# Attention and two feed-forward layers on one core: w_out2 rounded in layer 1, other tile addresses, the tail loaded sooner

## The chip, the core and the metric

The kernel runs on one NeuronCore of a Trainium2 chip, as one program. The time is the device time of one execution in microseconds; three executions of the kernel before took 1527.24, 1527.33 and 1527.49 us (median 1527.33). Beside them stands one profiled execution, from which all rows below come.

## The reference

The reference is a bidirectional softmax attention between tokens and a small state, and behind it two feed-forward layers. All is float32; the weights reach the kernel as 64-bit numbers, seen as pairs of 32-bit words.

```python
B, H, S, Ns, D = 8, 8, 512, 32, 64
xread = softmax(scale * x @ state.T) @ state        # for each of the 8 blocks and 8 heads
sread = softmax(scale * state @ x.T) @ x
x = concatenate([xread, sread], tokens)             # 8 * (512 + 32) = 4352 tokens of 512
h = x @ w_in;  x = maximum(0.01 * h, h) @ w_out     # layer 1, 2048 wide
g = x @ w_gate; x = (silu(g) * (x @ w_val)) @ w_out2   # layer 2, 1536 wide
```

## The kernel before

Every matmul of float32 numbers is made of three products of rounded parts: a number v is split into a high part h (ScalarE's `split_h`, line 161, a cast to fp32r) and a low part l = v - h (VectorE's `split_l`, line 164); `passes` (line 426) adds wl·vh, wh·vl and wh·vh in PSUM. The stationary operand of a matmul is a 128 x 128 tile, the moving one 128 x 512.

**Weights to float32.** `stage` (line 189) loads a tile `ws` of raw 64-bit weights, 512 KB. `to_f32` (line 204) gives six steps: scale and low on ScalarE, sign, limit, join and add on VectorE. `convert` (line 230) runs them over a list of keys, interleaved: for key n it issues scale(n), limit(n-1); low(n), sign(n); join(n-1); add(n-1) and the next load, in four steps, of which each `pump(1)` issues one. `finish2` (line 1080) takes each ready pair of keys of layer 2, makes the sums and splits that layer 2's products need (tiles `hl`, three buffers) and stores them to DRAM; each `pump_finish(1)` issues one of its steps.

**Layer 1** (from line 1296) works on 8 blocks j of 512 tokens and 16 column groups f, one iteration for each (j, f): `h_mm` (line 487), `h_act` (line 505: copy, leaky ReLU `hs`, split into `gh`, `gl`) and `y_mm` (line 524, with the products of two iterations before). Block 0 also converts layer 1's own weights. In blocks 1 to 6 each iteration pumps one step of `convert` and one of `finish2` over 24 keys of w_gate and w_val. The last block also carries the tail, the 256 state tokens, numbered block B: its weights come as `tail_in` and are split into `ch` and `cl` two iterations ahead (lines 1268 and 1272). There each iteration of TensorE is h_mm(B, f+1), h_mm(7, f+2), y_mm(7, f), y_mm(B, f), and six `convert` and five `finish2` steps are pumped. At f = 6 (`Y_SUMS`, line 1399) a loop drains what is left of both, the pool `prep` is closed, and layer 2's tiles are opened in its place: `load_w` fills 16 places `wq`, and `y_sums` (line 588) begins.

**Layer 2** (`layer2`, line 691) works on the 8 blocks in four pairs p. For the hidden values of a pair, seven products in Strassen's manner stand for eight (`quads`, line 752; `product`, line 696: six matmuls on one `wq` place). ScalarE copies the sums `C` out of PSUM and VectorE adds to them. `read_out` (line 866) multiplies the hidden values, split into `zh` and `zl` as stationary tiles, by the moving `wo` tiles of w_out2: 24 steps of 12 matmuls. Between the pairs p = 2 and p = 3 the `tail` (line 896) does the same for the 256 state tokens, with plain products: `hidden` and a read-out per f. w_out2 is converted within pair 0: `convert_o` (line 809) issues one of its four steps per key beside each product, loads the raw rows with two ahead, splits them, and stores the split parts (`wo_dram`) and the whole ones (`w2_dram["o", ...]`), which the tail loads and splits again.

**Order and addresses.** The kernel schedules by hand: each engine runs its instructions in the order in which the code issues them, and an instruction that waits holds all behind it on its engine. All loads and most stores go through SyncE's queue. Tiles of layer 2 come from `Places` (line 573), lists of named places; `take` asks for tiles aligned to 128 bytes.

In the built program of before, the sixteen `wq` places lie at byte 195072 and on, 2048 or 2176 apart; divided by 256, eight of their addresses leave 128 and eight leave 0. `zh` and `zl` leave 160. Layer 1's stationary tiles leave 128.

Of the kernel before, what the change touches and what calls it, by code (L numbers as in the profile page):

```python
# [9 lines left out]
F32 = mybir.dt.float32  # L10
# [15 lines left out]
def kernel(  # L26
# [123 lines left out]

    HF = NF2 // 2
    w2_dram = {
        (k, f): dram.tile([P, 2, 512], F32, name=f"w2_{k}{f}") for k in ("gate", "val", "o") for f in range(HF)
# [50 lines left out]
    def to_f32(key):  # L204
        t = staged.pop(key)
# [9 lines left out]
            "limit": lambda: nc.vector.tensor_scalar(  # L215
# [5 lines left out]
            "add": lambda: nc.vector.tensor_tensor(out=v, in0=v, in1=low3, op=ALU.add),  # L221
# [351 lines left out]
    class Places:  # L573
# [117 lines left out]
    def layer2(p2, ps2):  # L691
# [117 lines left out]
        def convert_o():  # L809

            places = {}

            def load(f):
                if f < NF2:
                    t, places[f] = wo_places.take("ws", [P, 512, 2], I32)
                    stage(("o", f), rows(w_out2, f), None, t)

            load(0)
            load(1)
            yield  # L820
            for f in range(NF2):
                v, tag = temps.take("raw")
                raw["o", f] = v
                ops = to_f32(("o", f))
                ops["scale"]()
                ops["low"]()
                ops["sign"]()
                yield
                ops["limit"]()
                ops["join"]()  # L830
                yield
                ops["add"]()
                wo_places.give(places.pop(f))
                hl, hl_tag = wo_places.take("hl")
                split_h(hl[:, 0].bitcast(F32R), v)
                load(f + 2)
                yield
                nc.sync.dma_start(out=w2_dram["o", f // 2][:, f % 2], in_=v)
                split_l(hl[:, 1].bitcast(F32R), v, hl[:, 0])
                yield  # L840
                nc.sync.dma_start(out=wo_dram[f // 2][:, f % 2], in_=hl)
                wo_places.give(hl_tag)
                temps.give(tag)

# [51 lines left out]
        def tail():  # L896
            n = widths[B]
            y = []
            for k in range(2):
                t, tag = temps.take("yr")  # L900
                nc.sync.dma_start(
                    out=t.rearrange("p (k c) -> p k c", k=2), in_=y_dram[B][:, 2 * k:2 * k + 2, :]
                )
# [6 lines left out]
            order = [(key, f) for f in range(NF2) for key in ("gate", "val", "o")]  # L910
            loads = iter(order)
            raw2 = {}

            def load2():
                key = next(loads, None)
                if key:
                    kind, f = key
                    a, b = (f // 2, f % 2) if kind == "o" else (f % HF, f // HF)
                    raw2[key] = wtiles[0].take("wraw")
                    nc.sync.dma_start(out=raw2[key][0], in_=w2_dram[kind, a][:, b])  # L920

            parts2 = {}
# [31 lines left out]

            for _ in range(4):
                load2()
            yield
            for kind in ("gate", "val"):
                split2(kind, 0)
                yield  # L960
# [507 lines left out]
```

## Time and profile before

| | |
|---|---|
| median of three runs | 1527.33 us |
| the profiled execution, its own time | 1526.71 us |
| its span, first to last instruction | 1524.9 us |
| TensorE busy | 1481.4 us (97%), 7114 matmuls |
| VectorE busy | 954.8 us (63%) |
| ScalarE busy | 688.7 us (45%) |
| GpSimd busy | 3.0 us, 8 instructions |
| granted TensorE clock, mean | 0.993 |
| stages | layer 1 to 702.7 us; pair 0 to 910, pair 1 to 1094, pair 2 to 1280, tail to 1337, pair 3 to the end |

In the profile's rows PE is TensorE, ACT ScalarE, DVE VectorE, POOL GpSimd and SP SyncE; "SPq" is its DMA queue. L432 is a line of the kernel; `out<-in` are the tiles that an instruction writes and reads. Times are from the span's start. A matmul's own time overlaps that of the next, so the pace is read from runs of many. In a row of waits, what ended the wait stands behind the arrow.

### The profile page before, as it was taken

What the parts mean: (1) busy time and instruction counts of PE and PEld (TensorE: products, weight loads), DVE (VectorE), ACT (ScalarE), POOL (GpSimd) and SP (SyncE); (2) the same over time, 40 slices, a digit from 0 to 9 for tenths busy, and PEclk for the clock granted to TensorE, in tenths of its full rate; (3) what the DMA queues carried; (4) which work ended last, traced back from release to release, by engine and by line L of the source; (5) the groups of instructions that cost most, each with busy time, mean ns of one, the idle gap of its engine ahead of it and who ended that gap; (6) DMA issues with size and microseconds to landing.
All of it is one profiled execution on the core that took longest, in us unless ns stands there. A gap on an engine that the chain in (4) does not pass through costs nothing.

```text
span 1524.9 us, 20092 instructions
## 1 busy us (share of the span) xinstructions
PE 1481.4 (97%) x7114; PEld 1158.6 (76%) x7114; DVE 954.8 (63%) x1728; ACT 688.7 (45%) x1246; POOL 3.0 (0%) x8
## 2 busy tenths in 40 slices
PE   6999999999999999999879999999999998999999
PEld 2446777777778778887658888888888887988887
DVE  6888688787877777865864534455344554744442
ACT  6777555555554545545433332333223333533322
POOL 0000000000000000000000000000000000000000
PEclk9999999999999999999999999999999999999999
DMA  8885444445453545664898666667666377576345
GB/s 296 291 302 173 139 153 158 145 173 178 135 176 116 190 138 183 249 218 167 297 309 301 224 235 202 190 214 238 224 190 189 101 242 251 180 257 191 118 146 186
DMA packets 146164, 307.53 MB, mean 202 GB/s; under 512 B 14608, under 2 KB 35088, under 8 KB 145040
## 3 DMA queue, kind: packets, MB, share of 16 engines
q1 hardware_dynamic: 144912, 297.85, 59.2%
q10 hardware_dynamic: 1152, 8.39, 1.3%
q8 instruction: 57, 0.93, 0.3%
q14 instruction: 43, 0.35, 0.1%
HBM read 228.59 MB, written 77.59 MB: 201 GB/s over the span
## 4 chain that ended last, share of the span: by engine, by line
PE 50%; DMA 4%; DVE 3%; ACT 1%; issue 1%; SPq 0%; ACTq 0%; DVEq 0%
PE ps_o L432 18%; PE ps_x L708 16%; PE ps_s L708 8%; PE ps_a L708 4%; PE ps_t L432 2%; PE ps_y L432 1%; DMA wo<-hl 1%; DMA ws<-in_dram 1%; PE ps_h L432 1%; DMA yr<-y_dram 1%; PE ps_yt L432 1%; DVE C L724 0%; DMA wraw<-w_gate 0%; ACT sg L728 0%; DVE hl L164 0%
## 5 line engine op out<-in xcount | busy, mean ns | idle before, releaser
L432 PE MATMUL ps_y<-gh,w_parts 128*128 128x512 f32 x1024 | 338.9, 391 | 0.0
L708 PE MATMUL ps_x<-yc,wq 128*128 128x512 f32 x1152 | 286.5, 396 | 14.9 <-DVE C L724 8.4
L708 PEld LDWEIGHTS ps_x<-yc,wq 128*128 128x128 f32 x1152 | 217.0, 189 | 67.9 <-DVE C L724 11.0
L432 PE MATMUL ps_o<-wo,zh 128*128 128x512 f32 x768 | 241.8, 396 | 0.0
L432 PEld LDWEIGHTS ps_y<-gh,w_parts 128*128 128x128 f32 x1024 | 192.2, 188 | 51.7 <-issue 8.1
L432 PE MATMUL ps_y<-gl,w_parts 128*128 128x512 f32 x512 | 199.5, 390 | 0.2 <-DVE gl L164 0.2
L432 PEld LDWEIGHTS ps_o<-wo,zh 128*128 128x128 f32 x768 | 144.3, 188 | 35.1
L432 PE MATMUL ps_o<-wo,zl 128*128 128x512 f32 x384 | 151.6, 395 | 2.4 <-DVE zl L164 2.4
L708 PE MATMUL ps_s<-yc,wq 128*128 128x512 f32 x576 | 149.6, 395 | 2.5 <-ACT C L720 2.5
L164 DVE TENSOR_TENSOR zl<-z,zh 128x512 fp32r<-128x512 f32 x96 | 66.3, 691 | 117.9 <-ACT zh L161 117.9
L161 ACT CAST gh<-hs 128x512 fp32r<-128x512 f32 (+1 forms) x144 | 85.9, 597 | 114.7 <-DVE hs L515 114.6
L164 DVE TENSOR_TENSOR gl<-hs,gh 128x512 fp32r<-128x512 f32 (+1 forms) x144 | 95.3, 662 | 57.4 <-ACT gh L161 54.6
L708 PEld LDWEIGHTS ps_s<-yc,wq 128*128 128x128 f32 x576 | 108.5, 189 | 27.9 <-ACT C L720 3.3
L161 ACT CAST zh<-z 128x512 fp32r<-128x512 f32 x96 | 59.1, 620 | 143.9 <-PE ps_o L432 143.8
L515 DVE SCALAR_TENSOR_TENSOR hs<-hs 128x512 f32<-128x512 f32 (+1 forms) x144 | 94.4, 656 | 31.3 <-ACT hs L514 30.2
L728 ACT ACTIVATE sg<-C 128x512 f32<-128x512 f32 x72 | 45.5, 632 | 148.1 <-DVE C L724 144.2
L514 ACT COPY hs<-ps_h 128x512 f32<-128x512 f32 (+1 forms) x144 | 80.5, 559 | 70.4 <-PE ps_h L432 69.2
L432 PEld LDWEIGHTS ps_y<-gl,w_parts 128*128 128x128 f32 x512 | 96.2, 188 | 20.1 <-DVE gl L164 0.5
L432 PE MATMUL ps_h<-ah,swl 128*128 128x512 f32 x256 | 106.5, 416 | 1.7 <-ACT hs L514 1.2
L432 PE MATMUL ps_h<-al,swh 128*128 128x512 f32 x256 | 100.4, 392 | 0.0
L432 PE MATMUL ps_h<-ah,swh 128*128 128x512 f32 x256 | 100.2, 391 | 0.0
L724 DVE TENSOR_TENSOR C<-ps_s,C 128x512 f32<-128x512 f32 x48 | 33.1, 690 | 106.0 <-PE ps_s L708 105.4
(128 smaller groups left out, 2023.8 us busy)
## 6 DMA issues: line engine op xcount, KB each, us to landing
wo<-wo SPq DMA_DIRECT2D x96, 512.0 KB, 4.5
wq<-quad_gate SPq DMA_DIRECT2D x168, 256.0 KB, 3.1
wq<-quad_val SPq DMA_DIRECT2D x168, 256.0 KB, 3.2
ws<-in_dram SPq DMA_DIRECT2D x68, 512.0 KB, 4.5
sw_dram<-sw SPq DMA_DIRECT2D x56, 256.0 KB, 3.0
sw<-sw_dram SPq DMA_DIRECT2D x56, 256.0 KB, 3.7
quad_gate<-hl SPq DMA_DIRECT2D x24, 512.0 KB, 4.5
quad_val<-hl SPq DMA_DIRECT2D x24, 512.0 KB, 4.1
```

The source lines that it names most:

```text
L161: nc.scalar.copy(dst, src)
L164: nc.vector.tensor_tensor(out=dst, in0=src, in1=hi.bitcast(F32), op=ALU.subtract)
L432: nc.tensor.matmul(ps, lhsT=w, rhs=v, start=first and n == 0, stop=last and n == len(todo) - 1)
L514: nc.scalar.copy(hs, ps[:, :n])
L515: nc.vector.scalar_tensor_tensor(out=hs, in0=hs, scalar=0.01, in1=hs, op0=ALU.mult, op1=ALU.max)
L708: nc.tensor.matmul(bank, lhsT=a, rhs=v, start=first and n == 0, stop=last and n == len(todo) - 1, skip_group_check=True,)
L724: nc.vector.tensor_tensor(out=kept[0], in0=bank, in1=kept[0], op=ALU.add)
L728: nc.scalar.activation(t[0], c, AF.Sigmoid)
```

## The change

w_out2's twelve row blocks become keys `("o", f)` at the end of layer 2's list in layer 1, so that `convert` and `finish2` handle 36 keys; the six row pairs get a branch of their own in `finish2`, which only splits and stores. `convert_o` and the whole parts in DRAM go. For layer 2's keys the steps limit and add run on GpSimd. Two pumps come twice as often. `Places` no longer aligns; a pad of 96 bytes ahead of `wpool`'s places, and the free choice in `p2`, give other addresses: in the built program all `wq` places, and `zh` and `zl`, now leave 128 over 256. The tail loads its input `yr` and its first weights at the start of pair 2's read-out, keeps three keys loaded ahead instead of four, and loads w_out2's two parts split.

```diff
@@ to_f32
+        engine = nc.vector if key[0] in ("in", "out") else nc.gpsimd
...
-            "limit": lambda: nc.vector.tensor_scalar(
+            "limit": lambda: engine.tensor_scalar(
...
-            "add": lambda: nc.vector.tensor_tensor(out=v, in0=v, in1=low3, op=ALU.add),
+            "add": lambda: engine.tensor_tensor(out=v, in0=v, in1=low3, op=ALU.add),
@@ Places.take
-            align = None if self.pool.space == bass.MemoryType.PSUM else 128
-            t = self.pool.tile(shape or self.shape, dtype, tag=tag, name=name, bufs=1, align_bytes=align)
+            t = self.pool.tile(shape or self.shape, dtype, tag=tag, name=name, bufs=1)
@@ quads
-        def quads(f, early, beside):
+        def quads(f, early):
             for n, step in enumerate(ORDER2):
-                next(beside, None)
@@
-        def convert_o():
...
@@ tail
+            order = [(key, f) for f in range(NF2) for key in ("gate", "val", "o")]
...
+                if kind == "o":
+                    h, ht = wtiles[0].take("wh", dtype=F32R)
+                    l, lt = wtiles[0].take("wl", dtype=F32R)
+                    for m, t in enumerate((h, l)):
+                        nc.sync.dma_start(out=t.bitcast(F32), in_=wo_dram[f // 2][:, f % 2, m])
+                    parts2[key] = (h, l), (ht, lt)
...
+            yr = []
+            for k in range(2):
+                yr.append(temps.take("yr"))
...
+            for _ in range(3):
+                load2()
+            yield
...
-            for _ in range(4):
-                load2()
-            yield
@@ layer2, the loop over pairs
-                if f == HF - 1 and not p:
-                    assert next(beside, 0) == 0
+                if f == HF - 2 and not p:
                     load_wo(4)
...
-                others.append(count(tail_steps, 6))
+                others = [count(tail_steps, 1), *others, count(tail_steps, 5)]
@@ the keys of layer 2, and finish2
+        keys2 += [("o", f) for f in range(NF2)]
...
+                if kind == "o":
+                    for n in range(2):
+                        hl = halves().rearrange("p a b c -> p a (b c)")
+                        split_h(hl[:, 0].bitcast(F32R), t[:, n])
+                        yield 1
+                        split_l(hl[:, 1].bitcast(F32R), t[:, n], hl[:, 0])
+                        yield 1
+                        nc.sync.dma_start(out=wo_dram[f // 2][:, n], in_=hl)
+                    finished[0] += 1
+                    continue
@@ layer 1, blocks 1 to 6
-                pump(f % 8 == 4)
-                pump_finish(f % 8 == 0)
+                pump(f % 4 == 2)
+                pump_finish(f % 4 == 0)
@@ the last block, f == Y_SUMS, behind load_w(WQ)
+                    wpool.tile([P, 24], F32, tag="pad", name="pad")
```

The order of instructions shows what this moves. First VectorE at the end of the drain of the last block, from the `cl` of f = 8 on. Before, the drain's rows between the second `gl` and the next `cl` are a few splits:

```order
L164 TENSOR_TENSOR cl<-tail_in,ch 128x512
L515 SCALAR_TENSOR_TENSOR hs<-hs 128x256
L164 TENSOR_TENSOR gl<-hs,gh 128x256
L515 SCALAR_TENSOR_TENSOR hs<-hs 128x512
L164 TENSOR_TENSOR gl<-hs,gh 128x512
L164 TENSOR_TENSOR hl<-hl 128x2x256 x2
L164 TENSOR_TENSOR hl<-two,hl 128x2x256 x2
L164 TENSOR_TENSOR swl<-sw,swh 128x512
L164 TENSOR_TENSOR cl<-tail_in,ch 128x512
```

Now (L215 is the sign, L221 the join, L165 `split_l`), the same `gl` and the eleven rows behind it are these:

```order
L165 TENSOR_TENSOR gl<-hs,gh 128x512
L215 TENSOR_SCALAR two<-ws 128x512
L221 SCALAR_TENSOR_TENSOR two<-ws,two 128x512
L165 TENSOR_TENSOR hl<-two,hl 128x512 x2
L215 TENSOR_SCALAR two<-ws 128x512
L221 SCALAR_TENSOR_TENSOR two<-ws,two 128x512
L215 TENSOR_SCALAR two<-ws 128x512
L165 TENSOR_TENSOR hl<-two,hl 128x512
L221 SCALAR_TENSOR_TENSOR two<-ws,two 128x512
L165 TENSOR_TENSOR hl<-two,hl 128x512
L215 TENSOR_SCALAR two<-ws 128x512
L221 SCALAR_TENSOR_TENSOR two<-ws,two 128x512
```

It goes on in this manner up to the next `cl`: 9 rows of L215, 10 of L221, 12 splits and a `swl` stand between that `gl` and that `cl`.

Second, SyncE in the same place, up to the first load of `yr` for layer 2. Before, it stores the last sums:

```order
L1119 DMA quad_gate_131<-hl 128x1024 x2
L1091 DMA w_val_119<-two 128x1024
L1263 DMA tail_in<-win_dram_106 128x4x128
L1109 DMA quad_val_137<-hl 128x1024
L1112 DMA quad_val_137<-hl 128x1024
L1119 DMA quad_val_137<-hl 128x1024 x2
L594 DMA yr<-y_dram_95 128x512
```

Now the loads of raw w_out2 (L194) and the stores of its parts (L1073) stand there in turns:

```order
L1104 DMA quad_val_131<-hl 128x1024 x2
L1248 DMA tail_in<-win_dram_106 128x4x128
L194 DMA ws<-in_dram 128x1024 x2
L1073 DMA wo_132<-hl 128x1024 x2
L194 DMA ws<-in_dram 128x1024 x2
L1073 DMA wo_133<-hl 128x1024 x2
L194 DMA ws<-in_dram 128x1024 x2
L1073 DMA wo_134<-hl 128x1024 x2
L194 DMA ws<-in_dram 128x1024 x2
L1073 DMA wo_135<-hl 128x1024 x2
L1073 DMA wo_136<-hl 128x1024 x2
L1073 DMA wo_137<-hl 128x1024 x2
```

All stores of w_out2's parts, and eight of its twelve loads, have moved behind layer 1's last stores of sums.

Third, ScalarE at the start of layer 2, from its first copy C. Before, the steps of w_out2 stand between the copies:

```order
L720 COPY C<-ps_x 128x512
L210 ACTIVATE ws<-ws 128x512
L211 ACTIVATE ws<-ws 128x512
L720 COPY C<-ps_s 128x512
L161 CAST hl<-raw 128x512
L720 COPY C<-ps_x 128x512
```

Now the copies follow each other:

```order
L722 COPY C<-ps_x 128x512
L722 COPY C<-ps_s 128x512
L722 COPY C<-ps_x 128x512
L722 COPY C<-ps_s 128x512
L722 COPY C<-ps_x 128x512
```

The 36 instructions of ScalarE for w_out2 have left pair 0.

## Rows read from the trace of the kernel before

**Rows 1.** The page's first part: busy time, share and instructions of each engine.
```profile
PE 1481.4 (97%) x7114; PEld 1158.6 (76%) x7114; DVE 954.8 (63%) x1728; ACT 688.7 (45%) x1246; POOL 3.0 (0%) x8
```

**Rows 2.** Waits of TensorE: who waited for whom, us in total, times, longest.
```profile
PE ps_x L708 <- DVE C L724: 8.4, 6, 3.2
...
PE ps_x L708 <- ACT C L720: 6.5, 2, 4.8
PE ps_t L432 <- DVE wl L164: 3.4, 1, 3.4
PE ps_h L432 <- DVE cl L164: 3.0, 3, 1.9
PE ps_s L708 <- ACT C L720: 2.5, 1, 2.5
...
PE ps_o L432 <- DVE zl L164: 2.4, 1, 2.4
```

**Rows 3.** The chain that ended last, in order of time: start, us, what.
```profile
657.58 3.06 PE ps_h L432 x18
...
674.82 2.72 PE ps_y L432 x12
...
681.80 2.72 PE ps_y L432 x12
...
702.73 1.40 PE ps_x L708 x6
...
845.57 64.44 PE ps_o L432 x276
...
1029.19 64.45 PE ps_o L432 x276
```

**Rows 4.** Groups of ScalarE from 704 to 800 us: busy, mean ns, idle before.
```profile
L210 ACT ACTIVATE ws<-ws 128x512 f32<-128x512 f32 x12 | 8.0, 669 | 13.3 <-DMA ws<-in_dram 13.3
...
L161 ACT CAST hl<-raw 128x512 fp32r<-128x512 f32 x12 | 7.4, 620 | 28.9 <-DVE raw L221 28.9
```

**Rows 5.** The chain from 1115 to 1142 us, in pair 2.
```profile
1121.38 1.38 PE ps_a L708 x6
1122.77 1.40 PE ps_x L708 x6
1124.17 1.37 PE ps_s L708 x6
```

**Rows 6.** SyncE's timeline from 1255 us; then a stretch's busy times, clock, DMA.
```profile
1282.26 0.73 SPq L920 DMA_DIRECT2D wraw<-w_o  x1
...
1283.00:1297.00 14.00, 10.63 (x58) 9.84 (x58) 7.89 (x16) 5.34 (x12) 0.00 (x0) 0.76 0.66 227
```

**Rows 7.** Timeline of VectorE from 622 us: start, us, what.
```profile
622.53 0.42 DVE L515 SCALAR_TENSOR_TENSOR hs<-hs 128x256 f32<-128x256 f32 x1
622.87 0.68 DVE L218 SCALAR_TENSOR_TENSOR two<-ws,two 128x512 int32<-128x512 int32 x1
623.47 0.42 DVE L164 TENSOR_TENSOR gl<-hs,gh 128x256 fp32r<-128x256 f32 x1
```

**Rows 8.** Groups of GpSimd over the span.
```profile
L1320 POOL MEMSET zero<- 128x512 f32 x1 | 0.5, 526 | 550.1 <-PE ps_r L399 550.1
masks.py:199 POOL TENSOR_SCALAR_AFFINE_SELECT ident<-ident 128x128 f32<-128x128 f32 x1 | 0.3, 292 | 0.1
masks.py:197 POOL MEMSET ident<- 128x128 f32 x1 | 0.2, 204 | 0.0
```

**Rows 9.** The page's DMA issues: KB each, median us to landing.
```profile
ws<-in_dram SPq DMA_DIRECT2D x68, 512.0 KB, 4.5
...
wo<-hl SPq DMA_DIRECT2D x12, 512.0 KB, 6.1
```

**Rows 10.** Timelines of VectorE and of TensorE behind the drain of before.
```profile
639.76 0.68 DVE L164 TENSOR_TENSOR cl<-tail_in,ch 128x512 fp32r<-128x512 f32 x1
...
643.12 0.69 DVE L164 TENSOR_TENSOR gl<-hs,gh 128x512 fp32r<-128x512 f32 x1 [0.68 <-ACT gh L161]
...
640.59 0.35 PE L432 MATMUL ps_h<-tailh,cl 128*128 128x256 f32 x1 [1.94 <-DVE cl L164]
```

More of the change, by code (lines that the diff above doesn't have):

```diff
@@ L152 @@
     w2_dram = {
-        (k, f): dram.tile([P, 2, 512], F32, name=f"w2_{k}{f}") for k in ("gate", "val", "o") for f in range(HF)
+        (k, f): dram.tile([P, 2, 512], F32, name=f"w2_{k}{f}") for k in ("gate", "val") for f in range(HF)
     }
@@ L807, in load_wo @@
                     nc.sync.dma_start(out=t.bitcast(F32), in_=wo_dram[f // 2][:, f % 2])
-        def convert_o():
[L811 to L819, printed above, removed]
-            yield
[L821 to L843, printed above, removed]
         zs = {}
@@ L897, in tail, with load2 @@
             n = widths[B]
+            order = [(key, f) for f in range(NF2) for key in ("gate", "val", "o")]
+            loads = iter(order)
+            raw2, parts2 = {}, {}
+            def load2():
+                key = next(loads, None)
+                if not key:
+                    return
+                kind, f = key
+                if kind == "o":
[4 more added lines that the diff above has]
+                    parts2[key] = (h, l), (ht, lt)
+                else:
+                    raw2[key] = wtiles[0].take("wraw")
+                    nc.sync.dma_start(out=raw2[key][0], in_=w2_dram[kind, f % HF][:, f // HF])
+            yr = []
+            for k in range(2):
+                yr.append(temps.take("yr"))
+                nc.sync.dma_start(
+                    out=yr[k][0].rearrange("p (k c) -> p k c", k=2), in_=y_dram[B][:, 2 * k:2 * k + 2, :]
+                )
+            for _ in range(3):
+                load2()
+            yield
             y = []
             for k in range(2):
[L900 to L903, printed above, removed]
+                t, tag = yr[k]
                 parts = wres.tile([P, 2, 2 * n], F32R, tag=f"wr{14 + k}", name="yt", bufs=1)
@@ L909, in tail @@
                 yield
[L910 to L922, printed above, removed]
             def split2(kind, f):
                 if f < NF2:
-                    t, tag = raw2.pop((kind, f))
-                    h, ht = wtiles[0].take("wh", dtype=F32R)
-                    l, lt = wtiles[0].take("wl", dtype=F32R)
-                    split_h(h, t)
-                    split_l(l, t, h)
-                    wtiles[0].give(tag)
+                    if kind != "o":
+                        t, tag = raw2.pop((kind, f))
+                        h, ht = wtiles[0].take("wh", dtype=F32R)
+                        l, lt = wtiles[0].take("wl", dtype=F32R)
+                        split_h(h, t)
+                        split_l(l, t, h)
+                        wtiles[0].give(tag)
+                        parts2[kind, f] = (h, l), (ht, lt)
                     load2()
-                    parts2[kind, f] = (h, l), (ht, lt)
             def hidden(f):
@@ L996, in first_z @@
                 split_z(f, h)
-        beside = convert_o()
         for p in range(len(pairs)):
@@ L1064, in next_load2 @@
                 k, f = key = loads2.pop(0)
-                stage(key, columns(w_gate if k == "gate" else w_val, f), prep)
+                stage(key, rows(w_out2, f) if k == "o" else columns(w_gate if k == "gate" else w_val, f), prep)
         twos, finished = [], [0]
```

3 lines of the change are left out of this document (1 added, 2 removed).

## The prediction

> **What bounds the kernel now.** The page's first part comes first: TensorE is busy for 1481.4 of 1524.9 us [rows 1], so a change can take away only what TensorE waits, or what each of its matmuls is too slow, and it can add waits. The waits of TensorE [rows 2] lie in three places. The first quarter of layer 2 waits for C, the copies and sums of ScalarE and VectorE: 8.4 + 6.5 + 2.5 = 17.4 us. The last block of layer 1 waits 3.0 us for cl, the low part of a tail weight, a VectorE result. The tail's start waits 3.4 us for wl and 2.4 us for zl. The chain in order of time [rows 3] then dates the stages: block pair 0 of layer 2 runs from 702.73 to 845.57 + 64.44 = 910.01, block pair 1, which has the same matmuls, from there to 1029.19 + 64.45 = 1093.64. All numbers are of this one execution of 1526.7 us; the median of the runs is 0.6 us above it. A measurement of this kernel can tell about 0.2%, 3 us, from no change.
>
> **Part 1: w_out2 leaves layer 2.** Pair 0 takes 207.3 us, pair 1 183.6 us. In pair 0 ScalarE's scale step waited 13.3 us for the loads of raw w_out2 and its casts 28.9 us for VectorE [rows 4], each time with copies of PSUM queued behind it. The order of ScalarE at the start of layer 2 shows that after the change only those copies are left. Bounds: the 17.4 us of named waits, and the whole difference of 23.7. I take -23, since pair 1 runs without one wait under the same load that pair 0 will then have.
>
> **Part 2: addresses.** Three products of six matmuls follow each other at 1121 to 1126 us, on the places at bytes 220800, 222976 and 225152 of the kernel before. Divided by 256 these leave 128, 0 and 128, and the products take 1.38, 1.40 and 1.37 us [rows 5]; eight of the sixteen places are of each kind. In layer 1 the stationary weights all leave 128, and twelve matmuls take 2.72 us, 0.227 each [rows 3]. In the read-out zh and zl leave 160, and 276 take 64.45 us, 0.2335 each. After the change all of them leave 128. Pair 1 without its 288 read-out matmuls is 183.6 - 67.2 = 116.4 us for 504, 0.231 each. With 0.228, as the 1.37 us say, 2016 matmuls gain 5.8 us; with 0.227, 1152 of the read-out gain 7.8. Bounds: nothing, if the address is not the cause, and 2016 x 0.004 + 7.8 = 16 us if all reach layer 1's pace. I take -13.5.
>
> **Part 3: the tail sooner.** The load of yr, and zl behind it, no longer ends late: 2.4 us. The other wait, 3.4 us, had a load that SyncE issued at 1282.26 or later, behind the stores of the read-out [rows 6]. The order of SyncE after the change has the load of val 1 behind these stores, and hidden(1) needs it soon, so this wait stays with another tile. The stretch from 1283 to 1297 has a granted clock of 0.76 [rows 6], 14 x 0.24 = 3.4 us lost at the lower level, 1.2 GHz; whether that goes with the smaller gap is open. Bounds: 0 and 2.4 + 3.4 + 3.4 = 9 us. I take -3. The o parts come split, 512 KB instead of 256 KB a step, under a steady 4.25 us of TensorE; I cost that at nothing, covered by the 3 steps of loading ahead.
>
> **Part 4: w_out2 and GpSimd in layer 1.** There are now 36 keys where there were 24. Through blocks 1 to 6 they are spread out, a step or two in each iteration. The place that matters is the last block at f = 6, where what is left is drained in one go. In the order of VectorE before, five instructions stood between a gl and the next cl; now 32: 9 signs, 10 joins, 12 splits (every one of w_out2) and a swl. TensorE needs that cl. Its queue holds behind it everything else of layer 1, and one step of 681.80 - 674.82 = 7.0 us in front of it [rows 3].
>
> How long is the drain? VectorE alone: short instructions follow each other at 0.34 us and long ones at 0.60 [rows 7], so with that cl 9 x 0.34 + 24 x 0.60 = 17.5 us. But a key's chain is longer. GpSimd's limit and add have no row. Its affine select, which reads and writes 128 elements, takes 0.29 us, a memset of 128 0.20 and one of 512 0.53 [rows 8]. The memsets give 0.10 us fixed, so an operation with one input at 512 is (0.29 - 0.10) x 4 + 0.10 = 0.88 us, and a second input adds 4 x 0.09, so 1.23 us. Bounds: 0.53 for either, and four times 0.29 for the limit, twice that for the add.
>
> In the drain key n + 1's sign stands ahead of key n's join, and key n + 1 is loaded into the buffer that the add of key n - 2 gives free. So from an add to the second one after it: load 4.5 us to landing [rows 9], scale 0.67 [rows 4], sign 0.42, join 0.68, add 1.23, and 0.2 for handing over: 7.7 us for two keys. The first two adds need no new load and end at 2.3 and 5.0 us; the ninth then ends at 2.3 + 4 x 7.7 = 33, the tenth 2.8 later (limit, join, add), then a cast 0.62 [rows 4], a split, swl and cl: 38.5 us. The stores of hl (three buffers, 6.1 us to landing [rows 9]) give 3 keys in some 10.7 us, about the same pace.
>
> The drain starts after the gl that ended 3.4 us behind the cl before [rows 10]; TensorE has 7.0 us to do. Wait: 3.4 + 38.5 - 7.0 = 34.9 us. What the same stretch loses now goes away: from 640.59 - 1.94 = 638.65, where TensorE could have begun [rows 10], to 657.58 [rows 3], two steps of 7.0 took 18.9 us, so 5. A wait of this length will leave TensorE at 1.2 GHz for a while, as the stretch after 1283 does [rows 6]: 2 us. Net +32. Bounds: with 17.5 us +11; with 50 us, rival 2, some +44. The limit and add of the other keys I cost at +1.5, from 0, if what VectorE no longer does covers them, to 8.
>
> Sum: -23 - 13.5 - 3 + 32 + 1.5 = -6. 1526.7 - 6 + 0.6 = **1521 us**.
>
> **Rivals.** *1, the drain is short.* If loads and stores keep ahead, the drain is VectorE's 17.5 us, part 4 becomes +11 + 1.5, and the time 1500. For it: most of the first keys' data is there when it starts. Against it: in the order of SyncE six of the twelve loads stand behind its stores.
>
> *2, slower: GpSimd and VectorE take turns.* No row of before shows the two at work together, since GpSimd has 8 instructions. If each of its operations kept VectorE out, a drained key would cost 1.9 us of VectorE (sign, join, split), 2.1 of GpSimd and some 1 us of loads not covered: 5 us, the drain 50 us and part 4 +44; the 26 keys before the drain would hold VectorE for another 55 us, of which I let 5 reach TensorE. The time is then 1526.7 - 39.5 + 49 + 0.6 = 1537. It decides from about 4.5 us per key on, where the sum is zero. The Trainium skill states such a rule in "SBUF — State Buffer", section "SBUF: two separate sides": VectorE instructions with two SBUF inputs and GpSimd share a port pair, held for a whole instruction, and the other engine blocks. By that rule, the sum would be the 1537 us just given; no run here shows it yet. The skill's "GPSIMD Engine Reference", section "Performance versus the Vector engine", gives 4497 ns for an add of 2048 elements, a quarter of which, as an estimate, is 1.1 us; with it the sum would be 1 us lower.
>
> *3, the address is not the cause.* Then part 2 is nothing: 1534.5 us. Against it: the pace alternates with the place, product by product, and layer 1 has the faster one throughout.
>
> *4, the change does not do what it says.* If pair 0 stays slow for another reason (the copies themselves), -23 shrinks to -17: 1527.
>
> **How the numbers follow.** Forecast 0.52, with an own range of 1509 to 1531 (8 us on the drain, 3 on the rest); rival 1 0.18; rival 2 0.20; rival 3 0.06; rival 4 0.04. The range takes in rivals 1 and 2 nearly whole: 1502 to 1537. Faster by over 3 us: rival 1 and some three quarters of the forecast, 0.57. Within 3 us: 0.18, from the forecast's upper part and rival 4. Slower: 0.25, rivals 2 and 3.
>
> **What would show it.** Pair 0 within 2 us of pair 1; no wait for C. Read-out runs of 276 at 62.7 us instead of 64.4. In the waits of TensorE one long wait of ps_h for cl near 650 us, some 35 us: under 20 makes part 4 wrong, and rival 1 right. In it, ScalarE waiting for ws and hl (loads, stores) speaks for my chain; VectorE and GpSimd each idle while the other runs, with long rows of GpSimd, for rival 2. One wait of about 3 us at the tail's start. If GpSimd's add takes over 2 us, the step that is wrong is its price.

## The result and the profile after

The kernel after took 1534.8 us (four executions, 1534.35 to 1535.46), the kernel before beside it 1527.41 us: 1.0053 of the time before, 95% interval 1.004 to 1.0067. That is slower by half a per cent, where the prediction had 1521 us and faster. The profiled execution has a span of 1532.6 us, 7.7 us more than before, at a granted clock of 0.981 instead of 0.993.

First the page's part 1 of the kernel after, then its waits of TensorE (us in total, times, longest); they answer to [rows 1, 2]:

```profile
PE 1462.9 (95%) x7114; PEld 1156.8 (75%) x7114; DVE 938.6 (61%) x1644; ACT 681.6 (44%) x1234; POOL 90.1 (6%) x80
```

```profile
PE ps_h L435 <- DVE cl L165: 39.3, 2, 38.9
...
PE ps_t L435 <- DVE wl L165: 6.3, 4, 2.7
PE ps_r L402 <- ACT et L394: 2.7, 2, 2.4
...
PE ps_h L435 <- ACT hs L517: 2.4, 2, 1.8
...
PE ps_y L435 <- ACT yst L558: 1.5, 2, 1.2
PE ps_y L435 <- DVE gl L165: 1.0, 2, 0.8
```

TensorE is busy 18.5 us less: its matmuls are quicker. The waits for C of pair 0 are gone, one long wait for cl has come, the tail waits four times instead of once, and ps_r, ps_h and ps_y wait in blocks 1 to 6, where [rows 2] have almost nothing. The chain in order of time dates the stages, as [rows 3] do for before:

```profile
694.38 5.46 PE ps_h L435 x18
...
749.03 1.39 PE ps_x L710 x6
...
757.22 1.36 PE ps_a L710 x6
...
866.02 62.56 PE ps_o L435 x276
...
1045.54 62.63 PE ps_o L435 x276
```

Layer 2 begins at 749.03 instead of 702.73 us: layer 1 is 46.3 us longer. Pair 0 then takes 866.02 + 62.56 - 749.03 = 179.6 us, pair 1 up to 1045.54 + 62.63 also 179.6; before they took 207.3 and 183.6. Taking each stage from its first matmul to the next one's, layer 1 has +46.3, pair 0 -27.7, pair 1 -4.0, pair 2 -6.3, the tail +3.4 and pair 3 -4.0: together +7.7 us, the difference of the spans.

The n-th matmul is the same in both programs, so the two traces can be laid side by side. At the end of block 6 (matmul 2840 of 7114) TensorE is 7.9 us behind the kernel before; in the last block this grows to 9.8, falls to 6.1 where short waits of the kernel before have no counterpart, is 44.5 right behind the drain's wait, and 46.3 at the start of layer 2. So layer 1's loss has two parts: 9.8 us ahead of the drain, nearly all of it in blocks 1 to 6, and 46.3 - 9.8 = 36.5 at the drain (its wait and the low clock behind it, less the short waits of before).

**The drain.** ScalarE's scale steps in it:

```profile
658.85 0.67 ACT L213 ACTIVATE ws<-ws 128x512 f32<-128x512 f32 x1 [3.45 <-DMA ws<-in_dram]
...
667.46 0.65 ACT L213 ACTIVATE ws<-ws 128x512 f32<-128x512 f32 x1 [2.55 <-DMA ws<-in_dram]
...
676.00 0.65 ACT L213 ACTIVATE ws<-ws 128x512 f32<-128x512 f32 x1 [2.87 <-DMA ws<-in_dram]
...
684.53 0.65 ACT L213 ACTIVATE ws<-ws 128x512 f32<-128x512 f32 x1 [2.97 <-DMA ws<-in_dram]
```

These are every second key, and each waits for its load (between them stands one more such wait): (684.53 - 658.85) / 3 = 8.6 us for two keys. Behind such a load the same turn goes on like this on VectorE (sign, a split, join):

```profile
676.68 0.43 DVE L215 TENSOR_SCALAR two<-ws 128x512 int32<-128x512 int32 x1 [3.55 <-ACT ws L213]
677.02 0.69 DVE L165 TENSOR_TENSOR hl<-two,hl 128x512 fp32r<-128x512 f32 x1
677.62 0.69 DVE L221 SCALAR_TENSOR_TENSOR two<-ws,two 128x512 int32<-128x512 int32 x1
```

From 655 to 694 us no engine is busy for half of the time, VectorE for 16.6, ScalarE for 15.4 and GpSimd for 18.9 of 39 us (the stretch: busy time of PE, PEld, DVE, ACT, POOL, then granted clock, DMA share, GB/s).

```profile
655.00:694.00 39.00, 0.46 (x4) 0.25 (x3) 16.62 (x30) 15.44 (x27) 18.85 (x18) 0.56 0.70 244
```

**Blocks 1 to 6.** GpSimd's groups over the span, then the timelines of GpSimd and of VectorE at one of its adds:

```profile
L224 POOL TENSOR_TENSOR two<-two,ws 128x512 int32<-128x512 int32 x36 | 55.5, 1542 | 438.7 <-ACT gh L162 196.2 <-DVE two L221 170.2 <-ACT hs L517 30.3
L218 POOL TENSOR_SCALAR ws<-ws 128x512 f32<-128x512 f32 x36 | 32.7, 909 | 162.3 <-DVE two L215 162.3
```

```profile
471.08 1.80 POOL L224 TENSOR_TENSOR two<-two,ws 128x512 int32<-128x512 int32 x1 [13.91 <-ACT gh L162]
472.85 1.08 POOL L218 TENSOR_SCALAR ws<-ws 128x512 f32<-128x512 f32 x1
```

```profile
471.03 0.69 DVE L165 TENSOR_TENSOR gl<-hs,gh 128x512 fp32r<-128x512 f32 x1
471.64 1.79 DVE L165 TENSOR_TENSOR hl<-hl 128x512 fp32r<-128x512 f32 x1
473.36 0.67 DVE L338 TENSOR_REDUCE r<-st 128x16 f32<-128x512 f32 x1
```

VectorE's split, 0.69 us in the row above it, takes 1.79 us while GpSimd adds, and GpSimd's add takes 1.80 where the shortest took 1.27. As I read it, each one's time holds the time for which the other held it up. The means fit; VectorE's groups from 160 to 630 us in the kernel after:

```profile
L165 DVE TENSOR_TENSOR gl<-hs,gh 128x512 fp32r<-128x512 f32 x100 | 76.2, 762 | 56.3 <-ACT gh L162 55.5
...
L165 DVE TENSOR_TENSOR al<-a,ah 128x512 fp32r<-128x512 f32 x12 | 10.4, 870 | 0.0
...
L322 DVE TENSOR_REDUCE m<-st 128x16 f32<-128x512 f32 x12 | 8.2, 686 | 0.4
```

and in the first experiment below, which has no GpSimd steps:

```profile
L165 DVE TENSOR_TENSOR gl<-hs,gh 128x512 fp32r<-128x512 f32 x101 | 69.9, 692 | 39.7 <-ACT gh L162 37.4
...
L322 DVE TENSOR_REDUCE m<-st 128x16 f32<-128x512 f32 x12 | 8.2, 686 | 0.4
...
L165 DVE TENSOR_TENSOR al<-a,ah 128x512 fp32r<-128x512 f32 x12 | 8.2, 684 | 0.0
```

These splits, with two inputs in SBUF, got longer, a reduction with one input did not. (Not every two-input group did: the join has 686 and 684 ns.)

**The tail.** SyncE in the kernel after:

```profile
1256.67 29.09 SPq L808 DMA_DIRECT2D wo<-wo  x12
1285.82 0.42 SPq L881 DMA_DIRECT2D wraw<-w_gate  x1
...
1290.06 0.59 SPq L881 DMA_DIRECT2D wraw<-w_val  x1
```

The first three weights are loaded early, but the fourth, gate 1, is issued only at 1285.82 us, behind twelve loads of `wo` that wait for their places, and val 1 behind the read-out's last stores.

### The profile page after: what moved, and what is told of

It is laid out like the page before. It is cut to its first block, busy times and chain, and to the rows that moved or that the text cites. A ratio compares the mean times of both kernels' runs of the same rounds, so it can differ in the third digit from the quotient of the medians.

```text
span 1532.6 us, 20186 instructions
## 1 busy us (share of the span) xinstructions
PE 1462.9 (95%) x7114; PEld 1156.8 (75%) x7114; DVE 938.6 (61%) x1644; ACT 681.6 (44%) x1234; POOL 90.1 (6%) x80
## 4 chain that ended last, share of the span: by engine, by line
PE 50%; DMA 4%; DVE 2%; ACT 1%; issue 1%; POOL 0%; SPq 0%; POOLq 0%; ACTq 0%; DVEq 0%
PE ps_x L710 17%; PE ps_o L435 16%; PE ps_s L710 9%; PE ps_a L710 4%; DMA wraw<-w_gate 2%; PE ps_y L435 1%; PE ps_h L435 1%; DMA ws<-in_dram 1%; PE ps_yt L435 1%; DVE wl L165 1%; DMA wo<-wo 0%; ACT wh L162 0%; POOL two L224 0%; DVE hs L518 0%; DMA wraw<-w_val 0%
## 5 line engine op out<-in xcount | busy, mean ns | idle before, releaser
L710 PE MATMUL ps_x<-yc,wq 128*128 128x512 f32 x1152 | 278.0, 389 | 0.0
L435 PE MATMUL ps_o<-wo,zh 128*128 128x512 f32 x768 | 236.6, 389 | 0.0
L165 DVE TENSOR_TENSOR gl<-hs,gh 128x512 fp32r<-128x512 f32 (+1 forms) x144 | 102.3, 710 | 75.4 <-ACT gh L162 74.0
L710 PE MATMUL ps_s<-yc,wq 128*128 128x512 f32 x576 | 146.1, 389 | 0.0
L165 DVE TENSOR_TENSOR zl<-z,zh 128x512 fp32r<-128x512 f32 x96 | 66.3, 691 | 115.7 <-ACT zh L162 115.7
L518 DVE SCALAR_TENSOR_TENSOR hs<-hs 128x512 f32<-128x512 f32 (+1 forms) x144 | 102.5, 712 | 21.3 <-ACT hs L517 20.1
```

The lines of the kernel that those rows point to most:

```text
L165: nc.vector.tensor_tensor(out=dst, in0=src, in1=hi.bitcast(F32), op=ALU.subtract)
L435: nc.tensor.matmul(ps, lhsT=w, rhs=v, start=first and n == 0, stop=last and n == len(todo) - 1)
L518: nc.vector.scalar_tensor_tensor(out=hs, in0=hs, scalar=0.01, in1=hs, op0=ALU.mult, op1=ALU.max)
L710: nc.tensor.matmul(bank, lhsT=a, rhs=v, start=first and n == 0, stop=last and n == len(todo) - 1, skip_group_check=True,)
```

## The experiments

The medians of the kernel before beside these runs lie between 1524.6 and 1525.5 us; each ratio is to those of its own group of runs.

### Limit and add back on VectorE

```diff
-        engine = nc.vector if key[0] in ("in", "out") else nc.gpsimd
+        engine = nc.vector
```

> The kernel after, with limit and add of layer 2's keys back on VectorE. Layer 1 of the kernel after falls 9.8 us behind the kernel before up to the last block's drain. Theory A, GpSimd's steps hold VectorE up: most of the 9.8 us goes (0 to 3 stay), and the wait of 38.9 us in the last block loses about 1 us in each of its 4 to 5 two-key cycles (an add of 0.7 instead of 1.5 us, a limit of 0.4 instead of 0.6): 1534.8 - 8 - 5 = 1522 us, 1519 to 1526. Rival B, the delay in blocks 1 to 6 comes from the additional conversion steps, whoever runs them: the 9.8 us stay or grow, since VectorE gets 72 more instructions; only the drain gets shorter: 1530 to 1537 us.

Measured: 1516.43 us, ratio 0.9937 (0.9923 to 0.9951). The first row of its waits of TensorE, and two scale steps of ScalarE in its drain, two keys apart:

```profile
PE ps_h L435 <- DVE cl L165: 33.5, 2, 32.7
```

```profile
643.07 0.69 ACT L213 ACTIVATE ws<-ws 128x512 f32<-128x512 f32 x1 [1.58 <-DMA ws<-in_dram]
...
650.65 0.67 ACT L213 ACTIVATE ws<-ws 128x512 f32<-128x512 f32 x1 [2.35 <-DMA ws<-in_dram]
```

Theory A, and by more than it said: at the end of block 6 TensorE is 0.7 us ahead of the kernel before, so the whole lag was GpSimd's doing, although VectorE has 72 instructions more. The denser steps alone, then, cost nothing up to there. The turn of two keys falls from 8.6 to 7.6 us. With the change's GpSimd steps alone undone, it would have been faster than before.

### The drain spread over blocks 1 to 6

```diff
-                pump(f % 4 == 2)
-                pump_finish(f % 4 == 0)
+                pump(f % 2 == 0)
+                pump_finish(1)
```

> The kernel after, with more frequent steps in blocks 1 to 6: the second convert step in every other iteration instead of every fourth, two finishing steps in every iteration; by a count of the steps nothing is left for the drain at f = 6. Theory A, the drain is a chain of loads and stores that TensorE waits for once and that hides when it is spread: the wait of 38.9 us and 3 us of low clock behind it go, and the 10 keys that move forward cost what the other 26 do (9.8 / 26 = 0.4 us each): 1534.8 - 42 + 4 = 1497 us, 1494 to 1506. Rival B, VectorE (busy 64 of 80 us in these blocks) has no room: each key moved costs TensorE its 3 us of VectorE and 2 us of GpSimd, 10 x 5 = 50 us, and the time stays near 1535 to 1543 us.

Measured: 1520.38 us, ratio 0.9968 (0.9955 to 0.998). Neither theory holds alone: the wait for the drain is gone (ps_h for cl is not among the longer waits), but TensorE is 34.1 us behind at the end of block 6. Whose fault that is, VectorE's load or GpSimd, the next three kernels tell.

### The same, with VectorE's steps, and with one of the two on GpSimd

```diff
-        engine = nc.vector if key[0] in ("in", "out") else nc.gpsimd
+        engine = nc.vector
...
+                pump(f % 2 == 0)
+                pump_finish(1)
```

> Both edits together: limit and add on VectorE, and the more frequent steps in blocks 1 to 6. Theory A (the 35 us that layer 1 lost in the kernel with spread steps are GpSimd's doing, and the drain is a chain that hides once spread): nothing of the 35 us in blocks 1 to 6, no drain: from 1516.4 us of the kernel with VectorE's steps its wait of 33.0 us and 2 to 3 us of low clock go, the ten keys moved forward cost 0 to 4: 1480 to 1485 us. Rival B (VectorE has no room for ten more keys in blocks 1 to 6, whoever runs limit and add): 10 keys x 4 us of VectorE cost TensorE up to 40 us there, 1500 to 1520 us.

Measured: 1490.11 us, ratio 0.9771 (0.9756 to 0.9786). Nearest to theory A (1480 to 1485), with more left in blocks 1 to 6 than it said: 6.9 us behind at the end of block 6, and no drain.

With limit alone on GpSimd, in the kernel with spread steps:

```diff
-            "add": lambda: engine.tensor_tensor(out=v, in0=v, in1=low3, op=ALU.add),
+            "add": lambda: nc.vector.tensor_tensor(out=v, in0=v, in1=low3, op=ALU.add),
```

> The kernel with spread steps (1520.4 us), with add on VectorE and only limit on GpSimd. Beside it one with only add on GpSimd. With neither some 1482 us, so there are 38 us to share. Theory A, VectorE is kept out for the whole of any GpSimd instruction: the price goes with GpSimd's busy time (limit 36 x 0.91 = 33 us, add 36 x 1.54 = 55 us): limit alone costs 14 us, 1496 us; add alone 24 us, 1506 us. Rival B, only an instruction with two inputs takes what VectorE needs: limit alone 1482 to 1485 us. Rival C, it is the handing over between two engines, two per key for either: each half, 1500 us.

Measured: 1495.99 us, ratio 0.9808 (0.979 to 0.9825). With add alone on GpSimd:

```diff
-            "limit": lambda: engine.tensor_scalar(
+            "limit": lambda: nc.vector.tensor_scalar(
```

> The kernel with spread steps, with limit on VectorE and only add on GpSimd. Theory A (price by GpSimd's busy time): 1506 us. Rival B (only an instruction with two inputs takes what VectorE needs): the whole price is the add's, 1515 to 1520 us. Rival C (handing over): 1500 us.

Measured: 1511.29 us, ratio 0.991 (0.9895 to 0.9925). GpSimd's group in either kernel:

```profile
L218 POOL TENSOR_SCALAR ws<-ws 128x512 f32<-128x512 f32 x36 | 27.8, 773 | 600.7 <-DVE two L215 334.5 <-DVE r L383 159.9 <-issue 69.5
```

```profile
L224 POOL TENSOR_TENSOR two<-two,ws 128x512 int32<-128x512 int32 x36 | 58.3, 1620 | 593.6 <-ACT gh L162 382.3 <-DVE two L221 108.7 <-ACT hs L517 43.3
```

Limit costs 1496.0 - 1490.1 = 5.9 us, add 21.2, both 30.3. Handing over (C) is out, since each is handed over as often. Limit, with one input, does cost, so B is out too; but per us of GpSimd's time it costs less (5.9 / 27.8 = 0.21) than add (21.2 / 58.3 = 0.36), so A holds in kind, not in its split. (The intervals of the two ratios leave some 3 us either way on the 5.9, so the 0.21 is rough.) In the kernel with limit alone the splits gl take 751 ns in the mean from 160 to 630 us, with VectorE's steps 693.

### GpSimd's steps in the kernel before

```diff
     def to_f32(key):
+        engine = nc.gpsimd if key[0] in ("gate", "val") else nc.vector
...
-            "limit": lambda: nc.vector.tensor_scalar(
+            "limit": lambda: engine.tensor_scalar(
...
-            "add": lambda: nc.vector.tensor_tensor(out=v, in0=v, in1=low3, op=ALU.add),
+            "add": lambda: engine.tensor_tensor(out=v, in0=v, in1=low3, op=ALU.add),
```

> The kernel before with one edit: limit and add of the 24 keys of w_gate and w_val on GpSimd; w_out2 stays in layer 2, addresses and tail as before. Theory A, GpSimd's instructions stretch VectorE's with two inputs, and TensorE loses 0.4 us per key (10.5 us over some 27 keys in the kernel after): 24 x 0.4 = 9 us slower, 0.6%, with the lag growing through blocks 1 to 6. Rival B, the loss needs the additional keys and the denser steps of the kernel after: 0 to 2 us slower.

Measured: 1529.88 us, ratio 1.0037 (1.0025 to 1.005), between the two. But the trace contradicts A: at the end of block 6 TensorE is not behind the kernel before at all (0.6 us ahead); it loses 4 us in the last block. From 160 to 630 us GpSimd has nearly the same work in both kernels, here 46 instructions and 58.6 us and in the kernel after 48 and 59.4 (second fence; GpSimd is the fifth pair):

```profile
160.00:630.00 470.00, 466.76 (x2591) 373.30 (x2589) 370.70 (x715) 251.84 (x468) 58.56 (x46) 1.00 0.47 159
```

```profile
160.00:630.00 470.00, 463.03 (x2550) 367.94 (x2549) 371.81 (x716) 251.90 (x469) 59.41 (x48) 1.00 0.48 163
```

That led to another theory: a threshold. From the two engines' timelines one can take, for each gl, the time from its end on VectorE to the first matmul that reads it. In the kernel before this lead is 5 to 6 us on the average of a block. The smallest lead in each kernel's blocks 1 to 5 (in block 6 all of them, the kernel before too, have one of 0.1), and how far TensorE is behind the kernel before at the end of block 6:

| kernel | smallest lead, us | behind, us |
|---|---|---|
| before | 2.6 | 0 |
| before, with GpSimd's steps | 1.4 | -0.6 |
| after, VectorE's steps | 1.4 | -0.7 |
| after | 0.1 | 7.9 |
| spread, VectorE's steps | 0.2 | 6.9 |
| spread, limit on GpSimd | 0.1 | 12.1 |
| spread, add on GpSimd | 0.1 | 25.2 |
| spread, both on GpSimd | 0.1 | 34.1 |

In these kernels, where a block leaves some lead, stretched instructions cost nothing; where it is used up, TensorE falls behind. But the lead of gl is a sign and not the place of the loss. One kernel below, without the added steps at the ends of blocks, keeps 1.3 us of it and is 4.0 us behind all the same. And of the 7.0 us that TensorE waits from 160 to 640 us in the kernel after, gl has 1.0; the other 6.0 are for results of ScalarE: et 2.7, hs 1.8 and yst, the copy of a block's outputs, 1.5. The longest of these waits, TensorE's and then ScalarE's part in it:

```profile
478.28 0.92 PE L402 MATMUL ps_r<-xn,et 128*32 128x64 f32 x32 [2.40 <-ACT et L394]
```

```profile
476.03 0.62 ACT L162 CAST ah<-a 128x512 fp32r<-128x512 f32 x1 [4.03 <-DVE a L343]
```

ScalarE makes et three instructions behind this cast, and the cast waits for a, which VectorE makes behind the split of 1.79 us shown above. In the first experiment, whose split takes 0.68 us in the same place, the cast waits 1.1 us less and TensorE not at all:

```profile
470.98 0.62 ACT L162 CAST ah<-a 128x512 fp32r<-128x512 f32 x1 [2.92 <-DVE a L343]
```

So 1.1 of the 2.4 us come down from GpSimd's add through VectorE and ScalarE to TensorE, where none of them has time in hand. The next kernel tests whether rarer steps leave that time.

### The kernel after, with the steps as rare as before

```diff
-                pump(f % 4 == 2)
-                pump_finish(f % 4 == 0)
+                pump(f % 8 == 4)
+                pump_finish(f % 8 == 0)
```

> The kernel after, GpSimd's steps and all, with the steps in blocks 1 to 6 as rare as before (1.125 instead of 1.25 an iteration), so that two keys more stay for the drain. Theory A, a threshold: gl is ready 3 to 6 us before the first matmul that reads it, and GpSimd's stretching costs nothing until that lead is used up in a block; at the old density (as in the kernel before with GpSimd's steps alone) it isn't: TensorE enters the last block 0 to 2 us behind the kernel before instead of 9, the wait for the drain grows by some 8 us to 45 to 49: 1532 to 1537 us in all. Rival B, each key that GpSimd handles costs TensorE some 0.4 us: 24 keys, 8 to 9 us behind at the last block, 1541 to 1545 us.

Measured: 1541.3 us, ratio 1.0104 (1.0089 to 1.0118). The total lies where B had it, but not for B's reason: TensorE is 0.1 us behind at the end of block 6, with a smallest lead of 1.4 us, as A says. So GpSimd's steps at the old density cost nothing up to there (-0.6 and 0.1 us in two kernels), the denser steps on VectorE neither (-0.7), and both together 7.9. All of the loss is the drain, whose wait A had put too low:

```profile
PE ps_h L435 <- DVE cl L165: 54.7, 3, 52.9
```

Two keys later in the drain, 14 us more, not 8: a pair of w_val whose sums and stores are then still to be made may be the rest; that was not tried.

### Two loads of the drain ahead

With VectorE's steps, and at f = 0 of the last block:

```diff
+                if f == 0:
+                    for tag in ("ah0", "al0"):
+                        key = loads2.pop()
+                        stage(key, rows(w_out2, key[1]), None, ab.tile([P, 512, 2], I32, tag=tag, name="ws"))
```

> The kernel after with limit and add on VectorE (wait of 33.0 us in the last block, 1516.4 us), and the raw rows of the last two keys of w_out2 loaded ahead, at the start of the last block, into two places that are free by then. Theory A, the drain goes at the pace of load, scale, sign, join, add, two keys in some 7 us: without the loads of two keys one such turn goes, the wait becomes 25 to 27 us, the time 1509 to 1511 us. Rival B, the pace is that of the stores of hl (three buffers, some 6 us to landing): the wait stays 31 to 33 us, 1515 to 1517 us. Rival C, VectorE's own 17.5 us plus what stands ahead: no change either, and VectorE is then busy throughout.

Measured: 1513.24 us, ratio 0.9926 (0.9913 to 0.9939). Its first row of the waits:

```profile
PE ps_h L435 <- DVE cl L165: 29.7, 1, 29.7
```

3.0 us less than the 32.7, between A and B. The loads do bear on the pace, but A forgot that a key whose load waits for nothing still takes its own 2 us of scale, sign, join, add: a turn of 7.6 us is replaced by some 4. The scale steps of the last three keys, the third last still waiting for its load:

```profile
660.79 0.65 ACT L213 ACTIVATE ws<-ws 128x512 f32<-128x512 f32 x1 [1.70 <-DMA ws<-in_dram]
...
662.58 0.69 ACT L213 ACTIVATE ws<-ws 128x512 f32<-128x512 f32 x1
...
664.43 0.69 ACT L213 ACTIVATE ws<-ws 128x512 f32<-128x512 f32 x1
```

### The addresses alone, in the kernel before

```diff
-            align = None if self.pool.space == bass.MemoryType.PSUM else 128
-            t = self.pool.tile(shape or self.shape, dtype, tag=tag, name=name, bufs=1, align_bytes=align)
+            t = self.pool.tile(shape or self.shape, dtype, tag=tag, name=name, bufs=1)
...
                     load_w(WQ)
+                    wpool.tile([P, 24], F32, tag="pad", name="pad")
```

> The kernel before, with the addresses alone changed (no alignment in Places, the pad of 96 bytes): all stationary tiles of layer 2 leave 128 over 256; the conversion of w_out2 stays in pair 0. Theory A, the address sets the pace: the 504 matmuls of a pair's products 0.227 instead of 0.231 us, 288 of its read-out 0.227 instead of 0.2335, so 4 us a pair, 16 us in all, 1511.5 us; the rows of six 1.36 us all alike, the read-out of 276 62.6 us. Rival B, the pace of the kernel after came from what else it changed: 1527 us. Between them: in pair 0, which waits for copies, a faster matmul only waits longer, 1513 us.

Measured: 1512.86 us, ratio 0.9909 (0.9893 to 0.9925); by the medians that is 12.6 us, and the span of the profiled execution is 16.6 us shorter. From its chain, pair 2's products, and the first read-out:

```profile
1112.91 1.36 PE ps_a L707 x6
1114.28 1.36 PE ps_x L707 x6
1115.63 1.36 PE ps_s L707 x6
```

```profile
843.63 62.56 PE ps_o L432 x276
```

Theory A. The products no longer alternate as in [rows 5], and the read-out has layer 1's pace. (The products' moving tiles leave 128 over 256 in both built programs, so it is the stationary tile's address that counts there.) Pair 0, still with w_out2 in it, takes 202.8 us here and 179.6 in the kernel after: 23.2 us is what w_out2 costs there.

### The tail

In the kernel before, `tail` of the kernel after alone:

```diff
+            for _ in range(3):
+                load2()
+            yield
...
-                others.append(count(tail_steps, 6))
+                others = [count(tail_steps, 1), *others, count(tail_steps, 5)]
```

> The kernel before with the tail of the kernel after alone (yr and three weights loaded at the start of pair 2's read-out, o parts loaded split). Theory A, read from the stages: the read-out of pair 2 gains the 2.4 us of its wait for zl, the tail loses 3.4 us since its fourth and fifth weight are loaded late: 1 us slower, -1 to +3. Rival B, as the prediction had it: 3 us faster.

Measured: 1528.85 us, ratio 1.0023 (1.0014 to 1.0033). Theory A: the read-out of pair 2 gains 2.3 us, the tail loses 3.5. Its waits name the place:

```profile
PE ps_t L432 <- DVE wl L164: 5.3, 2, 4.2
```

In the kernel after, five weights at the start instead of three:

```diff
-            for _ in range(3):
+            for _ in range(5):
                 load2()
...
-                    load2()
+                    if (kind, f) not in (("val", 1), ("o", 0)):
+                        load2()
```

> The kernel after, with five weights of the tail loaded at the start of pair 2's read-out instead of three, and the next load left out at the splits of val 1 and o 0, so that the number of places in use is as before. Theory A, the load of gate 1 (issued at 1285.82 us, behind twelve loads of wo that wait for their places) and of val 1 are late: the waits of 2.5 and 3.1 us for wl at the tail's start go, and some 1.5 us of the lower clock: the tail 61.2 -> 54 to 57 us, 1528 to 1531 us. Rival B, the tail is short of DMA throughput (its o parts come split, 512 KB instead of 256 KB a step): the waits come back some steps later, 1533 to 1536 us.

Measured: 1533.22 us, ratio 1.0051 (1.0038 to 1.0064), as good as no change against the 1.0053 of the kernel after. By the stages it lies between the theories: the tail takes 58.4 us instead of 61.2, but the read-out ahead of it 1.1 more. (With the same steps in the tail, eight other kernels here took 59.6 to 62.4 us for it.) The waits for gate 1 and val 1 are gone, so their late loads look like most of the 3.4 us; but gate 2 is now the first load behind the read-out's stores (issued at 1292.98 us), and one wait takes their place:

```profile
1301.08 0.51 PE L435 MATMUL ps_t<-yt,wl 128*128 128x256 f32 x1 [3.94 <-DVE wl L165]
```

### A faster kernel

VectorE's steps, spread, and the tail's w_out2 stored whole again, with four weights loaded ahead from the early start:

```diff
+                    nc.sync.dma_start(out=w2_dram["o", f // 2], in_=t)
...
-            for _ in range(3):
+            for _ in range(4):
```

> The two edits together, and w_out2 for the tail stored whole again: one load of 256 KB and two splits per step instead of two loads of 256 KB, four weights loaded ahead; the sooner start of the tail's loads stays. Theory A, the tail of the kernel after is short of loads (its stretch has a DMA share of 0.76 and waits of 5.4 to 6.3 us for wl; with three ahead): the tail takes 54 to 56 us instead of 61, 4 to 6 us below the kernel without this edit. Rival B, what is late is the first loads behind the read-out's stores, whatever their size: the waits stay, within 2 us of the kernel without this edit.

Measured: 1488.08 us, ratio 0.9756 (0.9741 to 0.9772), the fastest. The tail takes 57.9 us instead of the 61.6 of the same kernel without this edit: A in direction, short of its 54 to 56. Which of the two did it, the whole parts or the fourth weight ahead, was not taken apart. Part 1 of its page:

```profile
PE 1456.3 (98%) x7114; PEld 1153.3 (78%) x7114; DVE 950.5 (64%) x1728; ACT 686.0 (46%) x1246; POOL 3.0 (0%) x8
```

Two tries to save its last 7 us in blocks 1 to 6 missed. Without the added steps at the ends of blocks:

```diff
-                pump(f % 2 == 0)
-                pump_finish(1)
+                pump(f % 2 == 0 and 1 < f < 15)
+                pump_finish(1 < f < 15)
```

> The fastest kernel so far (1488.1 us) without the added steps in the first two and the last iteration of each block, where ScalarE has the block's outputs to copy. Theory A, the waits of TensorE in blocks 1 to 6 (ps_y for yst 4.1 us, ps_r for et 2.5 us, a lag of 7 to 8 us in all) come from these steps queued before the copies: 3 to 6 us less, 1482 to 1485 us, the steps moved still done before f = 6 of the last block. Rival B, what is left out there is done later in the block at the same price: within 1.5 us of 1488.

Measured: 1491.3 us, ratio 0.9779 (0.9765 to 0.9794): the lag grows to 4.0 us at the end of block 6, not to 6.7, but the steps left out come due in the last block, and layer 2 begins 7.3 us behind the kernel before instead of 2.3. With fewer steps in blocks 1 to 6 and more in the last:

```diff
-    PUMPS = [1, 1, 1, 1, 1, 1, 1]
+    PUMPS = [1, 1, 1, 2, 1, 1, 2]
...
+                pump(f % 8 in (1, 4, 6))
+                pump_finish(f % 8 in (0, 3, 5))
...
-                    pump_finish(5)
+                    pump_finish(7)
```

> The fastest kernel (1488.1 us) with fewer steps in blocks 1 to 6 (1.375 an iteration instead of 1.5, and 1.375 finishing steps instead of 2) and more in the last block (8 and 7 instead of 6 and 5 an iteration), so that at most a key is left at f = 6. Theory A (threshold): the lead of gl lasts through more blocks, and the lag of 7 to 8 us at the last block becomes 2 to 4: 1483 to 1486 us. Rival B, what blocks 1 to 6 save the last block pays, whose loads of raw rows give a key only every 3.9 us: 1487 to 1493 us.

Measured: 1508.44 us, ratio 0.9891 (0.9877 to 0.9905). The lag in blocks 1 to 6 is under 1 us, less than A's 2 to 4, and the last block pays: layer 2 begins 24 us behind, far more than B had. Two of its waits:

```profile
PE ps_h L435 <- ACT hs L517: 10.9, 5, 3.8
PE ps_h L435 <- DVE cl L165: 8.5, 3, 4.8
```

## Why the prediction failed

- *Part 1, -23:* right. Pairs 0 and 1 are equal to 0.1 us, no wait for C is left, and the addresses' run gives 23.2. Rival 4 is out.
- *Part 2, -13.5:* right, its size at the upper bound: 4 us a pair, 16 in all, and 16.6 alone in the kernel before by the spans, 12.6 by the medians. Rival 3 is out.
- *Part 3, -3:* wrong in sign, +1 (2.3 gained, 3.4 lost), and 1.0023 alone. The step that failed is "covered by the 3 steps of loading ahead". The prediction saw val 1 behind the stores of the read-out, but not gate 1 behind twelve waiting loads of `wo`; it costed one wait of 3 us, and there were four of 6.3 us in all. What the split o parts themselves add stays open: the engines of the DMA were busy for a share of 0.91 from 1286 to 1300 us, where [rows 6] have 0.66.
- *Part 4, the drain, +32:* the mechanism was right, the size some 4 us short: a wait of 38.9 instead of 34.9 us. The turn of two keys took 8.6 instead of 7.7 us: GpSimd's adds in it took 1.59 to 1.78 us and not 1.23, and a split of w_out2, 0.6 us, stands on VectorE between sign and join (677.02 us above), where the prediction's chain has none; the loads took 4.2 to 4.4 us instead of 4.5. ScalarE waits for `ws` seven times, 17.2 us in all, and for GpSimd only behind the last two adds, 4.7 us; on VectorE the drain still costs 32.7 us: rival 2's drain of 50 us did not come, nor rival 1's of 17.5.
- *Part 4, the other keys, +1.5:* this step failed, and it cost the most: without the 8.3 us too few the two spans would have been level (7.7 - 8.3 = -0.6). It cost 9.8 us, beyond its upper bound of 8, and going back to VectorE removes all of it. The lower bound was for a cover, "if what VectorE no longer does covers them"; but a shorter list for VectorE is no cover where the instructions that are left get longer, and ScalarE and TensorE wait for them with no time in hand.

The sum with the measured terms: pair 0 -27.7 + 4.0 = -23.7, addresses 4 x -4.0 = -16, tail -2.3 + 3.4 = +1.1, layer 1 +46.3, of which 9.8 are the other keys' and 36.5 the drain's: +7.7, the difference of the spans. Of the 13.8 us between forecast and time some 8.3 are the other keys, 4.5 the drain and its clock and 4.1 the tail; 3.2 came back from the addresses and pair 0.

Rival 2 had the other mechanism right and the place wrong: the two engines do take turns, but the price fell mostly on blocks 1 to 6, not on the drain, where VectorE has time. That its 1537 us come near the 1534.8 is in part luck: it had 44 for the drain and 5 for the other keys, and 36.5 and 9.8 were measured. The rule of the Trainium skill, "SBUF — State Buffer", section "SBUF: two separate sides" (a VectorE instruction with two SBUF inputs and a GpSimd one that reads SBUF exclude each other for a whole instruction), agrees with this trace: 0.69 us becomes 1.79 beside an add of 1.80, and reductions stay at 686 ns. What it costs TensorE here is nothing or 7.9 us up to the end of block 6, for nearly the same work of GpSimd.

The estimate from the Trainium skill's "GPSIMD Engine Reference", section "Performance versus the Vector engine", 1.1 us for the add, is near the shortest add here, 1.27 us; the mean was 1.54.

## What to carry to other kernels

Moving work to an idle GpSimd relieves VectorE by little where VectorE's instructions have two SBUF inputs: from 160 to 630 us it was busy for 371.8 us and not 379.7. Before doing it, measure how far ahead of their readers the results on the path are ready, those of the engines behind VectorE too; here the move cost nothing as long as that lead lasted. Work moved to an earlier stage needs a rate, not only a place: what is left for a drain is paid at the latency of its loads, with every engine idle for more than half of the time. And when loads are moved ahead, see which of them comes first behind the queue's next waiting transfer: that one is the late one.

## What was not expected of the hardware

- The byte address of a stationary tile sets the pace of float32 matmuls by 2 to 3%: 0.227 us with 128 over 256, 1.40 us per six (0.233) with 0, and 0.2335 with 160. It was read from [rows 3, 5] and then confirmed by a run that changed nothing but layer 2's addresses, 0.9%.
- The time for which VectorE or GpSimd is kept out stands in the profile as a longer instruction, not as a wait: of VectorE's waits from 160 to 630 us in the kernel after none names GpSimd. It shows in the mean of a group against the same group elsewhere (762 and 692 ns).
- A one-input GpSimd step (limit) holds up VectorE's two-input instructions as well, seemingly for less: some 0.21 us of TensorE per us of GpSimd where the add's were 0.36.
